# A weight conversion's closing integer addition on VectorE instead of GpSimd, in a fused attention and two-MLP kernel

## Chip, cores and metric

One core of a Trainium2 chip. The metric is the device time of one execution in microseconds: 691.84 us in the median of three runs before the change (691.09 to 692.73). Engines are named as in the profile: PE is TensorE, DVE is VectorE, ACT is ScalarE, POOL is GpSimd, SP is the engine that issues the DMAs.

## What is computed

Sliding-window attention with four sink columns, 2 batches x 8 heads x 768 positions x 64, then two MLPs over the 1536 tokens (512 -> 2048 -> 512 each) with two different activations. The MLP weights arrive as 64-bit floats.

```python
scores = scale * np.matmul(q, k.transpose(0, 1, 3, 2))
keep = is_sink | in_window                      # 4 sinks, window 128
a = softmax(np.where(keep, scores, -1e9))       # + 1e-9 in the denominator
x = np.matmul(a, v)                             # -> (1536, 512)
h = x @ w1_in                                   # first MLP
g = np.where(h >= 1, h, np.where(h <= -1, 0.0, (h + 1) ** 2 / 4.0))
x = g @ w1_out
h = x @ w2_in                                   # second MLP
g = h * np.clip(h + 3.0, 0.0, 6.0) / 6.0
out = g @ w2_out
```

## The kernel before

All data is kept transposed: features lie on the 128 partitions, tokens along the free dimension. Each matrix product of the MLPs is made of three passes on TensorE, because each operand is held as a high and a low part: high x high, high x low, low x high. The two parts are made by `high` (a copy that rounds to the matmul type, L139 to L145) and `low` (a DVE subtraction, L147 to L150).

The tokens are worked off in chunks (`CHUNKS`, L25): 512, 256, 256 and 512 tokens for the first MLP, three of 512 for the second. A chunk takes 16 steps, one per 128 of the 2048 hidden features (`FC`). In step s, `h_group(s)` (L537) makes 12 matmuls into one PSUM bank, then ACT and DVE apply the activation and split the result into gh and gl; two steps later `y_group` (L573) makes 12 matmuls of gh, gl and the output weights into four banks that accumulate over the 16 steps.

A weight tile is 128 x 512; there are 64: 16 for the way in and 16 for the way out of each MLP (raw0i, raw0o, raw1i, raw1o by the profile's names; 0 is the first MLP). A tile comes as 128 x 512 x 2 int32, the lower and upper words of the 64-bit floats. `narrow` (L179) makes an fp32 tile of it by integer work: L187 (ACT) or L185 (DVE) drops the sign of the upper word, L190 (DVE) clamps the value's range, L191 (DVE) takes the sign out of the upper word, L192 (DVE) shifts by 3 and puts the sign back, L195 (ACT) turns the lower word into a small number, and L196, the line that is changed, adds the two as integers. Two slots after `narrow`, `split` (L209) makes the high part (L143, ACT, or L145, DVE) and, a slot later, the low part (L150).

The order is set in three ways. PE and SP run in the order in which the program is written (`manual_schedule`, L630). For ACT, DVE and POOL, a planner orders the instructions. The program itself defers work: `defer(fn, slots)` keeps a function for so many slots, and `tick` (L126), which runs at each attention step and at each quarter of a step, calls those that are due; so the addition is written one slot after the rest of `narrow`. Where an operation can be made by ACT or DVE, `Balance` (L44) picks the engine whose account is less full; `bal.add` puts a known cost on an engine's account.

Attention is written as a list of small functions (`steps`), and `attend` calls them between the matmul groups: for chunk 0 before any MLP step, for the chunks 1 to 3 during the chunk before. The conversions of the first MLP's weights begin during the attention of chunk 0 (the way in runs eight steps ahead, `AHEAD`) and go on during chunk 0, one tile for the way in and one for the way out per step; the second MLP's are spread over chunk 3 of the first MLP and chunk 0 of the second (the queue of L608 to L615), as far as four raw buffers (`RAW`) and the weight tiles of the first MLP come free. After its conversion, an output-weight tile is written to DRAM (L213) and is read back by the later chunks (L227). The raw tile's last reader is L196, so SP's next load into that buffer (L173) waits for it.

Of the kernel before, what the change touches and what calls it, by code (L numbers as in the profile page):

```python
# [13 lines left out]
ALU = mybir.AluOpType  # L14
# [56 lines left out]
def f32(ap):  # L71
    return ap.bitcast(F32)
# [3 lines left out]
def sink_attention_moe_moe_kernel(  # L76
# [14 lines left out]
    nc = tc.nc  # L91
# [31 lines left out]
    def defer(fn, slots=1):  # L123
        waiting.append((clock[0] + slots, fn))
# [12 lines left out]
    bal = Balance()  # L137
# [41 lines left out]
    def narrow(t, dst):  # L179

        lo, hi = t[:, :, 0], t[:, :, 1]
        c = dst.bitcast(I32)
        n = c.shape[1]
        if bal.pick(dve=150 + n / 1.92, act=150 + n / 1.2) == "dve":
            nc.vector.tensor_scalar(out=c, in0=hi, scalar1=0x7FFFFFFF, scalar2=None, op0=ALU.bitwise_and)  # L185
        else:
            nc.scalar.activation(out=f32(c), in_=f32(hi), func=AF.Abs)  # L187
        bal.add("dve", 3 * 150 + 2 * n / 1.92 + n / 0.96)
        bal.add("act", 150 + n / 1.2)
        nc.vector.tensor_scalar(out=f32(c), in0=f32(c), scalar1=F64_LOW, scalar2=F64_HIGH, op0=ALU.max, op1=ALU.min)  # L190
        nc.vector.tensor_scalar(out=hi, in0=hi, scalar1=-(1 << 31), scalar2=None, op0=ALU.bitwise_and)  # L191
        nc.vector.scalar_tensor_tensor(  # L192
            out=c, in0=c, scalar=3, in1=hi, op0=ALU.logical_shift_left, op1=ALU.bitwise_xor
        )
        nc.scalar.activation(out=f32(lo), in_=lo.bitcast(U32), func=AF.Copy, scale=2.0 ** -51, bias=2.0)  # L195
        defer(lambda: nc.gpsimd.tensor_tensor(out=c, in0=c, in1=lo, op=ALU.add))  # L196

    def take(m, which, fc):

        t = raw.pop((m, which, fc))  # L200
        if which == "i":
            hi = wpool.tile([P, DM], F32R, tag=f"wih{fc}", name=f"wih{m}_{fc}")
            lo = wpool.tile([P, DM], F32R, tag=f"wil{fc}", name=f"wil{m}_{fc}")
            wi[m, fc] = (hi.rearrange("p (k f) -> p k f", f=P), lo.rearrange("p (k f) -> p k f", f=P))
        else:
            w = wo_tile(m, fc)
            hi, lo = w[:, 0, :], w[:, 1, :]

        def split(src):  # L209
            high(hi, src, DM)  # L210
            defer(lambda: low(lo, src, hi, DM))
            if which == "o":
                defer(lambda: nc.sync.dma_start(out=f32(wo_d[m][fc]), in_=f32(w.rearrange("p a f -> p (a f)"))), 4)  # L213

        if wide:
            t32 = raw_p.tile([P, DM], F32, tag="w32", name="w32", bufs=3)
            narrow(t, t32)
            defer(lambda: split(t32), 2)
        else:
            split(t)  # L220
# [409 lines left out]
    with tc.manual_schedule(engines={mybir.EngineType.PE, mybir.EngineType.SP}):  # L630
        nc.vector.memset(half, 0.5)
        make_identity(nc, ident)
        with ExitStack() as att:
# [17 lines left out]
            for s in range(len(seq) + LAG):  # L651
                lo = hi = fc = 0
                if s < len(seq):
                    ci, fc = seq[s]
                    m = chunks[ci][0]
                    if fast and ci + 1 < NCH:
                        lo, hi = ready[ci], ready[ci + 1]
# [65 lines left out]
```

## Time and profile before

| what | value |
|---|---|
| device time, median of 3 | 691.84 us (691.09 to 692.73) |
| the profiled execution's own time | 690.73 us |
| its span, from first to last instruction | 688.6 us |
| PE busy | 656.1 us, 95% |
| DVE busy | 429.2 us, 62% |
| ACT busy | 337.0 us, 49% |
| POOL busy | 97.7 us, 14% |
| mean granted clock of PE | 0.982 |
| chain that ended last | PE 78%, DVE 12%, DMA 6%, ACT 2% |

Busy time is the time in which an engine executes instructions. The chain is followed back from the last instruction: at each step to what released it, or to the instruction ahead of it on its engine. The profile's page has also the span in 40 slices with the busy share of each in tenths; DVE's line reads 5979998997765556553679999579322222222222, and POOL's 2311432332100000000113333133000000000000: there are two stretches in which both work.

### The profile page before, as it was taken

Reading aid. Unit: us, or ns where it says so; the run is one execution under the profiler, and the core shown is the slowest. Engines: PE = TensorE matmul, PEld = TensorE weight load, DVE = VectorE, ACT = ScalarE, POOL = GpSimd, SP = SyncE. Lnnn points to the kernel's source line nnn. Section 1 sums busy time; section 2 is a strip of 40 time slices with the busy share of each in tenths; the row PEclk is TensorE's granted clock in tenths of the full one; section 3 lists DMA queues with packets and bytes.
Section 4 is the critical chain, followed back from the end, with each engine's and each line's share of the span. In section 5 each row is a group of like instructions: output and inputs, shape, how many; then the busy total and the mean of one; then the engine's idle time right before and its main releaser. Section 6 shows DMA issues by size and latency. Waiting matters only on the chain.

```text
span 688.6 us, 9625 instructions
## 1 busy us (share of the span) xinstructions
PE 656.1 (95%) x3392; PEld 522.8 (76%) x3392; DVE 429.2 (62%) x968; ACT 337.0 (49%) x710; POOL 97.7 (14%) x83
## 2 busy tenths in 40 slices
PE   6889689989999999999999999999999999999997
PEld 3455457657788998888888887888888888888886
DVE  5979998997765556553679999579322222222222
ACT  6669756664454446554356566466232222222222
POOL 2311432332100000000113333133000000000000
PEclk9989889999999999999999999999999999999999
DMA  8135547834577465443199551994318332062321
GB/s 272 66 105 167 196 149 239 274 110 141 160 288 255 150 235 192 142 151 114 48 360 356 184 204 49 376 393 171 122 47 323 106 107 91 31 214 94 104 78 62
DMA packets 47024, 119.21 MB, mean 173 GB/s; under 512 B 4432, under 2 KB 15744, under 8 KB 46976
## 3 DMA queue, kind: packets, MB, share of 16 engines
q1 hardware_dynamic: 46976, 118.60, 49.5%
q8 instruction: 27, 0.44, 0.3%
q14 instruction: 21, 0.17, 0.1%
HBM read 92.36 MB, written 26.21 MB: 172 GB/s over the span
## 4 chain that ended last, share of the span: by engine, by line
PE 78%; DVE 12%; DMA 6%; ACT 2%; SPq 1%; issue 1%; POOL 0%; ACTq 0%; DVEq 0%; POOLq 0%
PE ps_y L589 34%; PE ps_h L545 34%; PE ps_v L421 5%; PE ps_s L321 3%; DVE w L192 2%; DMA raw0i<-moe_w_in_dram 2%; DVE w L190 2%; DMA raw0o<-moe_w_out_dram 1%; DVE p L328 1%; DVE wo L150 1%; PE ps_t L385 1%; PE ps_t L384 1%; DMA wo<-wo_d 1%; DVE wil L150 1%; DVE raw0i L191 1%; DVE p L342 1%
## 5 line engine op out<-in xcount | busy, mean ns | idle before, releaser
L589 PE MATMUL ps_y<-gh,wo 128*128 128x512 f32 (+1 forms) x896 | 268.8, 364 | 0.9 <-ACT pt L366 0.6
L589 PEld LDWEIGHTS ps_y<-gh,wo 128*128 128x128 f32 x896 | 163.5, 189 | 31.3 <-issue 4.6
L545 PE MATMUL ps_h<-xh,wih 128*128 128x512 f32 (+1 forms) x448 | 166.6, 372 | 11.0 <-DVE gl L150 11.0
L545 PE MATMUL ps_h<-xl,wih 128*128 128x512 f32 (+1 forms) x448 | 162.1, 362 | 0.4 <-DVE xl L150 0.4
L545 PE MATMUL ps_h<-xh,wil 128*128 128x512 f32 (+1 forms) x448 | 161.9, 361 | 0.0
L589 PE MATMUL ps_y<-gl,wo 128*128 128x512 f32 (+1 forms) x448 | 161.2, 360 | 0.0
L150 DVE TENSOR_TENSOR gl<-ps_h,gh 128x512 fp32r<-128x512 f32 (+1 forms) x112 | 68.6, 613 | 91.4 <-ACT gh L143 90.9
L143 ACT ACTIVATE gh<-ps_h 128x512 fp32r<-128x512 f32 (+1 forms) x112 | 60.0, 536 | 130.3 <-PE ps_y L589 91.8
L545 PEld LDWEIGHTS ps_h<-xh,wih 128*128 128x128 f32 x448 | 85.2, 190 | 31.6 <-DVE gl L150 13.0
L545 PEld LDWEIGHTS ps_h<-xl,wih 128*128 128x128 f32 x448 | 85.2, 190 | 12.8 <-DVE xl L150 0.9
L545 PEld LDWEIGHTS ps_h<-xh,wil 128*128 128x128 f32 x448 | 85.1, 190 | 12.9
L589 PEld LDWEIGHTS ps_y<-gl,wo 128*128 128x128 f32 x448 | 84.8, 189 | 12.0
L559 DVE SCALAR_TENSOR_TENSOR ps_h<-r,ps_h 128x512 f32<-128x512 f32 x48 | 33.4, 695 | 83.0 <-ACT r L558 82.9
L558 ACT ACTIVATE r<-ps_h,half 128x512 f32<-128x512 f32 x48 | 33.0, 688 | 87.5 <-PE ps_h L545 87.5
L347 ACT ACTIVATE p<-p,nm 128x260 f32<-128x260 f32 (+2 forms) x96 | 46.5, 485 | 30.1 <-DVE nm L328 29.5
L321 PE MATMUL ps_s<-kraw,qraw 64*128 64x260 f32 (+2 forms) x192 | 48.3, 475 | 13.2 <-DVE nm L328 7.3
L555 DVE SCALAR_TENSOR_TENSOR r<-r 128x512 f32<-128x512 f32 (+1 forms) x64 | 47.7, 745 | 14.9 <-ACT r L554 14.7
L196 POOL TENSOR_TENSOR w<-w,raw1i 128x512 int32<-128x512 int32 x16 | 24.8, 1547 | 209.6 <-ACT wih L143 145.6
L190 DVE TENSOR_SCALAR w<-w 128x512 f32<-128x512 f32 x64 | 40.1, 626 | 13.4 <-ACT w L187 13.3
L328 DVE CUSTOM_DVE_ANT_0 p<-ps_s,mask 128x260 f32<-128x260 f32 (+2 forms) x96 | 36.7, 398 | 17.0 <-PE ps_s L321 16.8
L321 PEld LDWEIGHTS ps_s<-kraw,qraw 64*128 64x128 f32 x192 | 23.4, 217 | 29.9 <-DVE nm L328 15.2
L554 ACT ACTIVATE r<-ps_h,half 128x512 f32<-128x512 f32 (+1 forms) x64 | 36.6, 571 | 15.9 <-PE ps_h L545 15.5
(60 smaller groups left out, 666.6 us busy)
## 6 DMA issues: line engine op xcount, KB each, us to landing
wo<-wo_d SPq DMA_DIRECT2D x80, 512.0 KB, 4.2
wo_d<-wo SPq DMA_DIRECT2D x32, 512.0 KB, 6.0
raw0i<-moe_w_in_dram SPq DMA_DIRECT2D x16, 512.0 KB, 5.5
raw0o<-moe_w_out_dram SPq DMA_DIRECT2D x16, 512.0 KB, 5.0
raw1i<-moe_w_in_dram SPq DMA_DIRECT2D x16, 512.0 KB, 5.9
raw1o<-moe_w_out_dram SPq DMA_DIRECT2D x16, 512.0 KB, 3.3
xh<-x2h_d SPq DMA_DIRECT2D x3, 1024.0 KB
xl<-x2l_d SPq DMA_DIRECT2D x3, 1024.0 KB, 9.3
```

What stands on the lines that cost most here:

```text
L143: nc.scalar.activation(out=dst, in_=src, func=AF.Copy)
L150: nc.vector.tensor_tensor(out=dst, in0=src, in1=f32(hi), op=ALU.subtract)
L190: nc.vector.tensor_scalar(out=f32(c), in0=f32(c), scalar1=F64_LOW, scalar2=F64_HIGH, op0=ALU.max, op1=ALU.min)
L321: nc.tensor.matmul(banks[e], tq[rows, u * P:(u + 1) * P], tk[rows, c0:c0 + w], start=True, stop=True)
L328: nc.vector.tensor_tensor_reduce(out=p[:, e, :], in0=banks[e], in1=masks[min(i, 2)], scale=-SCALE, scalar=BIG, op0=ALU.add, op1=ALU.min, a ...
L347: nc.scalar.activation(out=p[:, e, :], in_=p[:, e, :], func=AF.Exp, scale=-1.0, bias=nm[:, e:e + 1], accum_out=sm[:, e:e + 1],)
L421: nc.tensor.matmul(ps[e * D:(e + 1) * D, u0 * P:u1 * P], l, r, start=n == 0, stop=n == len(ops[0]) - 1)
L545: nc.tensor.matmul(ps, w[:, kc, :], x[:, kc, :], start=i == 0, stop=i == len(ops) - 1)
L554: nc.scalar.activation(out=r, in_=ps, func=AF.Relu, scale=0.5, bias=half)
L555: nc.vector.scalar_tensor_tensor(out=r, in0=r, scalar=1.0, in1=r, op0=ALU.min, op1=ALU.mult)
L559: nc.vector.scalar_tensor_tensor(out=ps, in0=r, scalar=1.0, in1=ps, op0=ALU.min, op1=ALU.mult)
L589: nc.tensor.matmul(ys[dm], a[:, cs], b, start=fc == 0 and i == 0, stop=fc == FC - 1 and i == 2)
```

## The change

The addition of L196 is issued to VectorE, and the planner's account of VectorE is charged for it. Nothing else is changed; the operands, the slot and all other lines are the same.

```diff
         nc.scalar.activation(out=f32(lo), in_=lo.bitcast(U32), func=AF.Copy, scale=2.0 ** -51, bias=2.0)
-        defer(lambda: nc.gpsimd.tensor_tensor(out=c, in0=c, in1=lo, op=ALU.add))
+        bal.add("dve", 160 + 1.3 * n)
+        defer(lambda: nc.vector.tensor_tensor(out=c, in0=c, in1=lo, op=ALU.add))
```

## Rows read from the trace of the kernel before

**Rows 1.** Table of two stretches: busy us (count) of PE, PEld, DVE, ACT, POOL

```profile
205.00:688.60 483.60, 478.80 (x2572) 400.85 (x2570) 254.78 (x523) 203.33 (x403) 43.33 (x29) 1.00 0.48 171
0.00:205.00 205.00, 177.34 (x823) 121.91 (x824) 174.39 (x446) 133.70 (x307) 54.37 (x54) 0.94 0.54 179
```

**Rows 2.** The same table, five stretches within the first 205 us

```profile
10.00:27.00 17.00, 14.19 (x40) 7.23 (x38) 16.19 (x50) 14.12 (x37) 4.43 (x4) 1.00 0.36 131
53.00:64.00 11.00, 9.90 (x54) 5.58 (x52) 10.65 (x38) 10.11 (x27) 2.67 (x2) 0.84 0.43 140
74.00:99.50 25.50, 16.54 (x65) 11.18 (x64) 25.14 (x47) 17.50 (x33) 10.58 (x8) 0.87 0.56 177
107.00:123.70 16.70, 16.48 (x78) 12.36 (x76) 15.86 (x30) 11.87 (x23) 5.91 (x4) 1.00 0.79 272
129.50:142.00 12.50, 8.40 (x40) 6.31 (x38) 12.50 (x25) 8.87 (x17) 5.40 (x4) 0.98 0.64 193
```

**Rows 3.** DVE instructions by line: count, duration ns minimum/median/maximum, start, forms

```profile
L190 DVE TENSOR_SCALAR w<-w x64: 400/421/1533, 10.9 to 477.8; 128x512 f32<-128x512 f32 x64
...
L192 DVE SCALAR_TENSOR_TENSOR w<-w,raw0i x16: 676/682/1774, 12.5 to 128.9; 128x512 int32<-128x512 int32 x16
...
L150 DVE TENSOR_TENSOR wil<-w,wih x32: 671/684/1806, 19.6 to 417.8; 128x512 fp32r<-128x512 f32 x32
...
L339 DVE TENSOR_SCALAR sm<-sm x48: 140/169/1274, 6.6 to 312.6; 128x2 f32<-128x2 f32 x48
...
L559 DVE SCALAR_TENSOR_TENSOR ps_h<-r,ps_h x48: 680/696/697, 424.4 to 677.5; 128x512 f32<-128x512 f32 x48
```

**Rows 4.** Timeline of POOL and DVE: start us, us, engine, line, instruction

```profile
17.38 1.29 POOL L196 TENSOR_TENSOR w<-w,raw0i 128x512 int32<-128x512 int32 x1 [2.77 <-ACT wih L143]
...
17.45 1.77 DVE L192 SCALAR_TENSOR_TENSOR w<-w,raw0i 128x512 int32<-128x512 int32 x1
...
79.60 0.68 DVE L192 SCALAR_TENSOR_TENSOR w<-w,raw0o 128x512 int32<-128x512 int32 x1
...
80.20 0.68 DVE L555 SCALAR_TENSOR_TENSOR r<-r 128x512 f32<-128x512 f32 x1
```

**Rows 5.** Table of stretches for line L196 alone: POOL busy us and (count)

```profile
0.00:205.00 205.00, 50.99 (x35) 0.94 0.54 179
...
330.00:500.00 170.00, 43.33 (x29) 1.00 0.62 229
```

**Rows 6.** DVE by line and form, 0 to 205 us, last row 205 to 330 us

```profile
L190 DVE TENSOR_SCALAR w<-w 128x512 f32<-128x512 f32 x35 | 22.4, 639 | 10.6 <-ACT w L187 10.6
...
L150 DVE TENSOR_TENSOR wo<-w,wo 128x512 fp32r<-128x512 f32 x16 | 14.3, 893 | 0.0
...
L192 DVE SCALAR_TENSOR_TENSOR w<-w,raw0i 128x512 int32<-128x512 int32 x16 | 13.5, 846 | 0.0
...
L150 DVE TENSOR_TENSOR wil<-w,wih 128x512 fp32r<-128x512 f32 x16 | 12.6, 788 | 0.0
...
L342 DVE TENSOR_SCALAR p<-p,sm 128x260 f32<-128x260 f32 x32 | 11.9, 413 | 0.1
...
L339 DVE TENSOR_SCALAR sm<-sm 128x2 f32<-128x2 f32 x30 | 9.1, 305 | 2.1 <-ACT p L347 2.0
...
L342 DVE TENSOR_SCALAR p<-p,sm 128x260 f32<-128x260 f32 x32 | 10.3, 352 | 0.5
```

**Rows 7.** Chain of waits within the first 205 us: start us, us, engine, tile, line

```profile
13.60 1.29 DVE w L190
...
138.39 0.85 DVE w L190
```

**Rows 8.** Waits in the first 205 us: who waited for whom, us, times, longest

```profile
ACT wo L143 <- POOL w L196: 9.9, 9, 3.0
...
PE ps_h L545 <- DVE gl L150: 10.3, 4, 5.9
...
SPq L173 <- POOL w L196: 20.0, 9, 4.8
```

## The prediction

> **What bounds the kernel now.** I read the page first, then a table of stretches, the chain of waits, and last the DVE instructions by kind. In the table of two stretches the reader sees where PE's idle time is: from 205 us on PE is busy for 478.80 of 483.60 us, before that for only 177.34 of 205.00 [rows 1]. So 27.7 us of idle time lie in the first 205 us, in which the first layer's weights are converted beside attention, and 4.8 us in all the rest. In the rest the chain is matmuls behind matmuls, 2.72 us per dozen once attention is over. Nothing that DVE saves there can show, as long as it keeps up.
>
> In the first 205 us DVE is busy for 174.39 us [rows 1], and the chain runs along DVE in long pieces. Five stretches of this kind, from 10, 53, 74, 107 and 129.5 us on, are 82.7 us in sum, and DVE is busy in 80.34 of them [rows 2]. Here VectorE's own work decides, and here 64 more instructions for VectorE look like a bad idea.
>
> What speaks for the change is how long DVE's instructions are. L190, the clamp, takes 421 ns in the median and up to 1533; L192 682 and up to 1774; the low half of a weight (L150, wil) 684 and up to 1806; even L339, on two columns, 169 and up to 1274 [rows 3]. The long ones lie beside a GpSimd addition: the one that starts at 17.38 runs 1.29 us, to 18.67, and L192, which starts at 17.45, takes 1.77 us instead of 0.68 and ends at 19.22, about its own usual time after the addition [rows 4]. It did not run slower, it stood still. L559, which reads one of its operands from PSUM, takes 680 to 697 ns in all 48 cases [rows 3], six of them beside an addition.
>
> The Trainium skill states this as a rule ("SBUF — State Buffer", Who interferes with whom): VectorE and GpSimd share a pair of ports, and the second to start waits for the whole of the first's instruction, where VectorE's is in a two-port mode or has two inputs in SBUF and GpSimd's reads SBUF. By that rule each stall goes with its addition, and the stall in the trace agrees.
>
> **What the change removes.** It removes 64 GpSimd additions, 35 of them before 205 us, of 50.99 / 35 = 1.46 us in the mean [rows 5], and the stalls that they cause. I size these by kind for the first 205 us: count times (mean there less undisturbed length) [rows 3, 6]. L190: 35 x (639 - 421) = 7.6 us. L339: 30 x (305 - 169) = 4.1. L150 wo: 16 x (893 - 684) = 3.3. L192 of raw0i: 16 x (846 - 682) = 2.6. L342 of 260 columns: 32 x (413 - 352, its mean from 205 to 330 us, where GpSimd is idle) = 2.0. L150 wil: 16 x (788 - 684) = 1.7. That is 21.3 us; L555, L191 and the narrower L342 bring it to about 27, worked out in the same way: 0.77 us per addition.
>
> **What it adds.** One VectorE instruction per weight tile, with two int32 tiles of 128x512 in SBUF as inputs. The trace has no such DVE addition. The nearest rows are L192 (int32, two SBUF inputs, 682 ns) and L150 (fp32, two SBUF inputs, 684) [rows 3], and I take 0.68 us. From below it is bounded by L190's 0.42 us with one input [rows 3], from above by the 1.46 us of the same addition on GpSimd. An instruction occupies the engine for less than its length, as the next starts before it ends: the 0.68-us ones at 79.60 and 80.20 are 0.60 apart [rows 4]. So 35 x 0.60 = 21 us come and 27 go, and DVE gets 6 us freer before 205 us. At the bounds (0.34 or 1.38 us occupied) it would be 15 us freer or 21 us fuller.
>
> **What of it is on the path.** In the five stretches led by DVE, 22 additions start (4 + 2 + 8 + 4 + 4) [rows 2]: 22 x 0.60 = 13.2 us are added to the chain. The chain now holds 18 stretched DVE pieces there; the first and the last are L190 at 13.60 with 1.29 us and at 138.39 with 0.85 us, against 0.34 undisturbed [rows 7]. Their excess is 16.5 us, 0.92 each. So these stretches shrink by 16.5 - 13.2 = 3.3 us. Outside of them two stretched L190 and one addition on GpSimd leave the chain and some three of DVE's join it, which I set at 0.5 us. The sum is 3.8 us.
>
> From 330 to 500 us the other 29 additions go the same way [rows 5]. A step of the first layer needs of DVE, undisturbed, L190 0.42 + L191 0.42 + L192 0.68 + the addition 0.68 + the low half 0.68 + three instructions of 0.69 for g (L555, L556, L150) = 4.95 us, and PE needs 2 x 2.72 = 5.44 us for that step. The cover is thin, 0.49 us, but the stalls that fill it now leave. I cost this part at nothing; without the cover 29 x 0.60 = 17 us are at stake.
>
> **The planner's account.** `bal.add` charges VectorE 826 ns per tile, which pushes choices to ScalarE. They are there already: all copies of L143 run on ACT, and of the 64 first steps of a conversion 63 are ACT's (L187) and one is DVE's (L185). At most that one moves, 0.4 us.
>
> **The hand-over.** Today GpSimd starts 0.13 to 0.23 us after L192's end and takes 1.46 us, so the sum is there some 1.7 us after L192. ScalarE waits for it, 9.9 us in 9 places for wo before 205 us [rows 8]. On VectorE it is there 0.7 us after L192 if it follows at once. L195 doesn't hold it up: it ended before L192 in all 64 cases. DVE's queue may: it is worked off in order, and the addition is written one step later than L192, so that L328, L342, gl or a second tile's L190 to L192 may stand between, and these stand behind it in turn; PE and ACT wait for them. SP's loads of raw tiles wait 20.0 us for the addition, which reads a raw tile last [rows 8]; that wait turns into one for VectorE, and SP's order stays.
>
> The sum is made against the profiled execution: 690.73 - 3.8 = 686.9 us. The median of the runs shown, 691.84, lies 1.1 us higher, so I name 688.0 us.
>
> **Rivals.** (a) Transfers and PE's own order hide it. Between the stretches the chain passes through loads of raw tiles that SP issues only once PE has freed an attention buffer; if those are fixed in time, DVE is only earlier at a wait. For it: four of the stretches border on such a load. Against it: what SP waits for there is PE, and PE was held up by DVE before. Time: within 1.4 us of 691.8. Chance 0.18.
>
> (b) Slower: the addition sits late in DVE's order. ACT works in order too, so a copy that waits for the sum blocks gh and the exponentials behind it. It decides from the point where over 1.0 us (1.7 less 0.7) of other DVE work stands between L192 and the addition: two instructions of 0.60, or L190, L191 and L192 of a second tile (0.34 + 0.34 + 0.60 = 1.28). If each of the 22 tiles then costs 0.4 us more, that is 8.8 us, less the 3.8 gained: 697. If DVE's stalls had another cause than GpSimd, only the 13.2 us would remain: 705. For it: DVE has work in its queue nearly always in these stretches. Against it: GpSimd has nothing left that DVE could stand still for. Chance 0.22.
>
> The Trainium skill has a rule on the side of (b) ("Perfetto Trace Analysis", Optimizing Scalar/DVE Operations): where VectorE is saturated, moving work to ScalarE or even GpSimd may make sense; this change does the reverse. The same paragraph warns that it might not help between VectorE and GpSimd, for their shared port, and the stall shown above is a case of that warning.
>
> (c) More than forecast: all 27 us of stalls count, a part of the additions falls into DVE's idle time (30.6 us before 205), and PE's wait for gl, 10.3 us in 4 places [rows 8], shrinks with them: 8 to 10 us, so 682 to 684. Chance 0.10.
>
> **How the numbers follow.** The forecast has 0.50 (684.5 to 690.4), (a) 0.18, (b) 0.22, (c) 0.10. About 0.2%, 1.4 us, is what a measurement of this kernel can tell from no change. Faster by more: 0.50 + 0.10 = 0.60; within it: 0.18; slower: 0.22. The range goes from 681.5, just past (c), to 696, up to the milder half of (b).
>
> **What would show it.** Right: L190, L192, L150 with w and L339 all within 0.1 us of their medians; 64 DVE additions of 0.66 to 0.70 us; DVE's busy time, 429 us, down by 48 (27 before 205 us and some 21 after 330, sized alike) and up by 64 x 0.60 = 38, to about 420; PE's idle time in the first 205 us down by 3 to 5 us; PE without gaps after 330 us. Wrong: longer additions; ACT's wait for the sum above 15 us; a new PE wait for gl in 330 to 500 us. The prediction falls if DVE gets freer and the first 205 us do not get shorter.

## Result: 1.5% faster, two to three times what was forecast

The changed kernel takes 680.30 us in the median of four runs (678.59 to 683.12), beside 692.09 for the kernel before. The ratio on record is 0.9854, with a 95% interval of 0.9819 to 0.9889. It isn't the quotient of these two medians (0.983); it is that to some 690.4 us, where the kernel before lay in two later series (690.24 and 690.42). A comparison on another occasion, six runs of it, gave 682.51 beside 689.38 us, ratio 0.9882 (0.9845 to 0.9918). So the change takes 7 to 12 us off; 3.8 were forecast. The median of 680.3 lies 1.2 us below the range; the ratio, applied to the 691.84 us on which the forecast stands, gives 681.7, at its lower edge.

The profiled execution took 683.12 us (span 681.3), the longest of the four. The page's busy times, to be read beside those of the table before:

```profile
PE 657.6 (97%) x3392; PEld 523.7 (77%) x3392; DVE 415.9 (61%) x1031; ACT 336.4 (49%) x711; POOL 3.4 (0%) x19
```

DVE's busy time fell from 429.2 to 415.9 us although it has 64 instructions more (1031 against 968; the one at L185 has gone to ACT). POOL is left with 3.4 us. The instructions of [rows 3], in the same columns, and the addition, which now stands on L197 and is issued as a custom instruction on 16-bit halves:

```profile
L190 DVE TENSOR_SCALAR w<-w x64: 406/422/430, 11.3 to 470.1; 128x512 f32<-128x512 f32 x64
...
L192 DVE SCALAR_TENSOR_TENSOR w<-w,raw0i x16: 673/686/692, 12.9 to 129.5; 128x512 int32<-128x512 int32 x16
...
L150 DVE TENSOR_TENSOR wil<-w,wih x32: 668/686/694, 18.4 to 409.4; 128x512 fp32r<-128x512 f32 x32
...
L197 DVE CUSTOM_DVE_ANT_0 w<-raw0i,w x16: 679/686/690, 14.6 to 132.7; 128x1024 uint16<-128x1024 uint16 x16
```

The stalls are gone to the last one: L190's longest is 430 ns where it was 1533. The addition takes 0.69 us, as its nearest rows had it (0.68). By kind, for the first 205 us (columns as in [rows 6]; L339 is now L340):

```profile
L190 DVE TENSOR_SCALAR w<-w 128x512 f32<-128x512 f32 x35 | 14.8, 422 | 11.9 <-ACT w L187 11.8
...
L150 DVE TENSOR_TENSOR wo<-w,wo 128x512 fp32r<-128x512 f32 x16 | 11.0, 687 | 0.6 <-ACT wo L143 0.6
...
L340 DVE TENSOR_SCALAR sm<-sm 128x2 f32<-128x2 f32 x31 | 5.0, 163 | 2.0 <-ACT p L348 1.9
```

The clamp fell from 639 to 422 ns in the mean, the low half of wo from 893 to 687, L339 from 305 to 163. PE idles 19.0 of the first 205 us instead of 27.7 [rows 1]:

```profile
0.00:205.00 205.00, 185.98 (x879) 128.79 (x880) 169.64 (x496) 136.14 (x318) 3.38 (x19) 0.93 0.58 192
```

The waits that answer to [rows 8]:

```profile
PE ps_h L546 <- DVE gl L150: 5.0, 3, 3.7
...
ACT wo L143 <- DVE w L197: 2.9, 2, 2.0
...
SPq L173 <- DVE w L197: 29.8, 9, 6.8
```

ACT's wait for the sum of a wo tile went from 9.9 to 2.9 us and PE's for gl from 10.3 to 5.0. SP's wait for the raw tile's last reader grew from 20.0 to 29.8 us. SP comes to that point earlier: over the 16 steps its waits for PE, at the attention loads that it issues in between (L290 and L302 before), fell from 75.4 to 49.6 us.

The place of the gain is best seen with the span cut at the first matmul of a step: the start (up to step 0), the 16 steps of chunk 0, the 32 of chunks 1 and 2, the next 24 (chunk 3 and half of the chunk after it), and the rest. Before (columns as in [rows 1]: stretch, length, then PE, PEld, DVE, ACT, POOL, clock, DMA):

```profile
0.00:68.30 68.30, 55.90 (x240) 30.75 (x240) 55.79 (x204) 49.08 (x136) 15.17 (x28) 0.93 0.46 153
68.30:192.50 124.20, 108.94 (x505) 80.18 (x504) 109.75 (x221) 77.24 (x155) 37.65 (x25) 0.95 0.58 187
192.50:332.50 140.00, 139.69 (x1091) 120.87 (x1090) 79.11 (x267) 71.28 (x188) 1.54 (x1) 1.00 0.53 183
332.50:461.60 129.10, 128.36 (x578) 106.38 (x577) 108.71 (x170) 74.95 (x129) 35.24 (x23) 1.00 0.67 251
461.60:688.60 227.00, 223.25 (x985) 184.57 (x984) 75.82 (x110) 64.48 (x103) 8.09 (x6) 1.00 0.35 122
```

After:

```profile
0.00:74.10 74.10, 62.29 (x241) 33.71 (x241) 56.44 (x222) 52.20 (x141) 3.38 (x19) 0.82 0.43 142
74.10:185.10 111.00, 104.05 (x505) 77.95 (x504) 98.62 (x235) 72.31 (x149) 0.00 (x0) 0.98 0.63 205
185.10:325.10 140.00, 139.74 (x1092) 120.89 (x1091) 80.61 (x270) 71.98 (x190) 0.00 (x0) 1.00 0.53 185
325.10:454.40 129.30, 128.41 (x579) 106.44 (x578) 105.53 (x192) 75.00 (x128) 0.00 (x0) 1.00 0.67 250
454.40:681.30 226.90, 223.16 (x985) 184.67 (x983) 74.75 (x117) 64.87 (x104) 0.00 (x0) 1.00 0.35 122
```

The last three stretches differ by 0.0, 0.2 and 0.1 us. The 16 steps fell from 124.2 to 111.0 us, and the start got longer, 68.3 to 74.1. PE's idle time in the 16 steps went from 15.3 to 7.0 us, and PE was then busy for 94% of them. The other 4.9 us of the 13.2 are PE's busy time, 108.94 to 104.05 us for the same number of matmuls, at a granted clock of 0.98 instead of 0.95.

### The profile page after: what moved, and what is told of

Read it like the earlier page. It is cut to its first block, busy times and chain, and to the rows that moved or that the text cites. A ratio compares the mean times of both kernels' runs of the same rounds, so it can differ in the third digit from the quotient of the medians.

```text
span 681.3 us, 9471 instructions
## 1 busy us (share of the span) xinstructions
PE 657.6 (97%) x3392; PEld 523.7 (77%) x3392; DVE 415.9 (61%) x1031; ACT 336.4 (49%) x711; POOL 3.4 (0%) x19
## 4 chain that ended last, share of the span: by engine, by line
PE 74%; DVE 11%; DMA 9%; ACT 3%; issue 1%; SPq 1%; ACTq 0%
PE ps_y L590 32%; PE ps_h L546 31%; DMA raw0i<-moe_w_in_dram 4%; PE ps_s L322 4%; PE ps_v L422 4%; DVE w L192 2%; DMA raw0o<-moe_w_out_dram 2%; DVE w L197 2%; DMA raw1o<-moe_w_out_dram 1%; PE ps_t L386 1%; DMA raw1i<-moe_w_in_dram 1%; PE ps_t L385 1%; ACT w L187 1%; PE ps_k L397 1%; DVE p L329 1%
## 5 line engine op out<-in xcount | busy, mean ns | idle before, releaser
L590 PEld LDWEIGHTS ps_y<-gh,wo 128*128 128x128 f32 x896 | 163.1, 189 | 31.5 <-issue 4.4
L590 PE MATMUL ps_y<-gl,wo 128*128 128x512 f32 (+1 forms) x448 | 160.9, 359 | 0.0
L150 DVE TENSOR_TENSOR gl<-ps_h,gh 128x512 fp32r<-128x512 f32 (+1 forms) x112 | 68.7, 613 | 87.4 <-ACT gh L143 87.3
L546 PEld LDWEIGHTS ps_h<-xl,wih 128*128 128x128 f32 x448 | 84.9, 190 | 11.8
L322 PE MATMUL ps_s<-kraw,qraw 64*128 64x260 f32 (+2 forms) x192 | 50.0, 495 | 11.4 <-DVE nm L329 6.9
L329 DVE CUSTOM_DVE_ANT_0 p<-ps_s,mask 128x260 f32<-128x260 f32 (+2 forms) x96 | 36.8, 401 | 20.0 <-PE ps_s L322 19.8
L555 ACT ACTIVATE r<-ps_h,half 128x512 f32<-128x512 f32 (+1 forms) x64 | 36.7, 573 | 17.6 <-PE ps_h L546 17.1
L556 DVE SCALAR_TENSOR_TENSOR r<-r 128x512 f32<-128x512 f32 (+1 forms) x64 | 35.4, 554 | 15.5 <-ACT r L555 15.4
L190 DVE TENSOR_SCALAR w<-w 128x512 f32<-128x512 f32 x64 | 27.0, 422 | 17.1 <-ACT w L187 16.9
L557 DVE TENSOR_TENSOR ps_h<-ps_h,r 128x512 f32<-128x512 f32 (+1 forms) x64 | 35.9, 562 | 0.8
```

The lines of the kernel that those rows point to most:

```text
L150: nc.vector.tensor_tensor(out=dst, in0=src, in1=f32(hi), op=ALU.subtract)
L322: nc.tensor.matmul(banks[e], tq[rows, u * P:(u + 1) * P], tk[rows, c0:c0 + w], start=True, stop=True)
L329: nc.vector.tensor_tensor_reduce(out=p[:, e, :], in0=banks[e], in1=masks[min(i, 2)], scale=-SCALE, scalar=BIG, op0=ALU.add, op1=ALU.min, a ...
L546: nc.tensor.matmul(ps, w[:, kc, :], x[:, kc, :], start=i == 0, stop=i == len(ops) - 1)
L555: nc.scalar.activation(out=r, in_=ps, func=AF.Relu, scale=0.5, bias=half)
L556: nc.vector.scalar_tensor_tensor(out=r, in0=r, scalar=1.0, in1=r, op0=ALU.min, op1=ALU.mult)
```

## Experiments

Three theories stood against each other. **A**: the gain is that VectorE no longer stands still beside GpSimd. **B**: it is the planner's new order of DVE and ACT, which differs from the old one almost from the start. **C**: it is the hand-over, the sum and the raw tile being there sooner.

**The stalls put back, everything else kept (e1, e9).** After the VectorE addition GpSimd adds the sum to itself into a tile that nobody reads. In the programs, DVE's and ACT's instructions stand in the changed kernel's order one by one.

```diff
+        def add():
+            nc.vector.tensor_tensor(out=c, in0=c, in1=lo, op=ALU.add)
+            nc.gpsimd.tensor_tensor(out=spill, in0=c, in1=c, op=ALU.add)
+
+        defer(add)
-        defer(lambda: nc.vector.tensor_tensor(out=c, in0=c, in1=lo, op=ALU.add))
```

> The changed kernel, with one GpSimd addition more per weight tile: when VectorE has made the sum, GpSimd adds the sum to itself into a tile that nobody reads (same shape and type as the addition of the kernel before). The order of VectorE's and ScalarE's instructions is the changed kernel's, instruction for instruction. Theory A (the gain is that VectorE no longer stands still): the stalls come back, some 0.77 us per addition, 27 us on DVE before 205 us, of which 16.5 us lay on the chain: 680 + 16.5 = 697 us, and at least 688. Theory B (the gain is the planner's new order of DVE and ACT): the order is unchanged, so 680 us within 2. Theory C (the gain is that the sum is there sooner and the raw tile is released sooner): both are kept, so 680 us within 2.

Measured: 703.59 us (700.37 to 706.76), ratio 1.0193 (1.0148 to 1.0237) to the kernel before; that is 6.6 us over the 697 expected. e9 is the same with `[:, 0:2]` on the three operands of GpSimd's addition.

> As e1_pool_beside, but GpSimd's extra addition reads and writes 2 of the 512 columns. Waits, semaphores and the order of DVE and ACT are those of e1_pool_beside; only the length of GpSimd's work differs. Theory A (what costs is DVE standing still for as long as GpSimd works): some 0.1 to 0.2 us per addition, so 680 to 685 us. Rival (what made e1_pool_beside slow, 703.6 us, is the further reader of the sum, that is, buffers released later, and semaphores): 698 us or more.

Measured: 680.11 us (678.94 to 682.25), ratio 0.9868 (0.9817 to 0.9920). At one and the same order, with the same waits, 64 GpSimd additions of 512 columns (1.17 us in the mean) cost 703.59 - 680.11 = 23.5 us more than 64 of 2 columns (0.35 us). That is theory A, and B and C are out as explanations of this cost. The later release of the sum's tile is no cause either: in e1 ACT waits for GpSimd's addition once, for 0.5 us, in the whole span. The 23.5 us are not DVE's lost time alone, as PE's clock falls with it (see the table below). One stall in e1, on the timeline (start, length; L193 is L192 of the kernel before):

```profile
87.33 1.04 POOL L200 TENSOR_TENSOR spill<-w 128x512 int32<-128x512 int32 x1 [4.04 <-DVE w L199]
...
87.10 0.68 DVE L150 TENSOR_TENSOR gl<-ps_h,gh 128x512 fp32r<-128x512 f32 x1
87.70 1.21 DVE L193 SCALAR_TENSOR_TENSOR w<-w,raw0o 128x512 int32<-128x512 int32 x1
```

GpSimd works from 87.33 to 88.37. L193, with two inputs in SBUF, starts at 87.70 and ends at 88.91, half a microsecond later than it would. The gl subtraction, which reads one input from PSUM, keeps its 0.68 us beside the same addition, but it had started first. The trace of the kernel before shows the case in which GpSimd starts first:

```profile
96.86 1.58 POOL L196 TENSOR_TENSOR w<-w,raw0o 128x512 int32<-128x512 int32 x1 [4.78 <-DVE w L192]
97.23 0.68 DVE L150 TENSOR_TENSOR gl<-ps_h,gh 128x512 fp32r<-128x512 f32 x1
...
372.99 1.54 POOL L196 TENSOR_TENSOR w<-w,raw1i 128x512 int32<-128x512 int32 x1 [3.42 <-DVE w L192]
373.27 1.81 DVE L555 SCALAR_TENSOR_TENSOR r<-r 128x512 f32<-128x512 f32 x1
```

Ten gl subtractions of 512 columns start there with over 1.1 us of a GpSimd addition still to come, and none takes more than 0.69 us; of twelve L555, as large but with both inputs in SBUF, eleven take 1.79 to 1.81 us, and the twelfth stands beside an addition that itself takes 2.15 us instead of some 1.3. In both traces, 91 of the 93 DVE instructions that start within an addition and are over 0.1 us longer than usual are so by what GpSimd had left at their start, less 0.12 to 0.14 us. Where the difference lies, in the profiled executions of e1 and then of e9, which are 27.7 us apart (start, 16 steps, 24 steps):

```profile
0.00:76.80 76.80, 60.34 (x241) 32.08 (x241) 60.97 (x212) 51.30 (x139) 14.55 (x29) 0.87 0.42 137
76.80:202.50 125.70, 110.66 (x505) 81.46 (x504) 115.68 (x246) 76.25 (x153) 29.80 (x25) 0.93 0.55 182
...
342.00:477.00 135.00, 130.82 (x578) 107.29 (x578) 116.51 (x192) 74.63 (x128) 25.27 (x23) 0.99 0.65 239
```

```profile
0.00:69.70 69.70, 55.98 (x240) 30.75 (x240) 54.45 (x216) 50.13 (x138) 6.18 (x29) 0.90 0.46 150
69.70:181.10 111.40, 104.73 (x504) 77.64 (x503) 100.79 (x242) 74.24 (x154) 8.83 (x24) 0.98 0.62 205
...
321.10:450.10 129.00, 128.35 (x578) 106.40 (x577) 105.37 (x192) 74.92 (x128) 7.24 (x22) 1.00 0.68 251
```

The start differs by 7.1 us, the 16 steps by 14.3, the 24 steps by 6.0. The last is the thin cover of the prediction: with additions and stalls on DVE at once, the steps beside PE's 5.44 us no longer fit, and PE waits 4.1 us there for gl. Without the stalls it holds to about 1 us (129.0 to 129.5 us with the change, 129.1 before, 128.1 in e2 with no addition).

**No addition at all (e2), and two (e3).** e2 leaves the lower words out.

```diff
-        nc.vector.tensor_scalar(out=hi, in0=hi, scalar1=-(1 << 31), scalar2=None, op0=ALU.bitwise_and)
+        nc.vector.tensor_scalar(
+            out=hi, in0=hi, scalar1=-(1 << 31), scalar2=-(1 << 30), op0=ALU.bitwise_and, op1=ALU.bitwise_xor
+        )
...
-        defer(lambda: nc.gpsimd.tensor_tensor(out=c, in0=c, in1=lo, op=ALU.add))
```

> The kernel before without the addition on any engine: the lower words are left out, and the exponent is put right in L191 by a second bitwise operation instead. Neither GpSimd's stalls nor VectorE's additions are there. Theory A: against the changed kernel DVE has 21 us less before 205 us, of which 13 lie on the path: 680 - 13 = 667 us, and in any case below 680. Theory B: an order of its own, anywhere between 680 and 695. Theory C: the sum is there at once, so faster than 680 too, but DVE's busy time tells nothing of it.

Measured: 671.20 us (668.10 to 673.76), ratio 0.9722 (0.9686 to 0.9758), 4 us over the 667 of theory A. So GpSimd's additions cost the kernel before 690.24 - 671.20 = 19.0 us, waits for the sum included, and VectorE's cost the changed kernel 680.30 - 671.20 = 9.1 us; by the two intervals each is good to some 3 us.

e3 adds `nc.vector.tensor_tensor(out=spill, in0=c, in1=c, op=ALU.add)` behind the changed kernel's addition.

> The changed kernel with a second VectorE addition per tile, the sum with itself into a tile that nobody reads. It prices an addition of 0.60 us on VectorE. By the prediction's sum (22 of 35 on the path) 13.2 us more than the changed kernel, 693 us; if all 35 before 205 us count, 21 more, 701; if VectorE isn't what decides in the first 205 us, 680 within 2. The planner orders DVE and ACT anew here, which may add or take some us.

Measured: 691.09 us (688.80 to 693.75, ten runs), ratio 1.0010 (0.9992 to 1.0028): the second addition costs 10.8 us. That is less than the 13.2 of the sum on which it was tested, though not by more than the noise. e2 (start, 16 steps), then e3 (start, 16 steps, 24 steps):

```profile
0.00:63.90 63.90, 54.53 (x241) 30.12 (x241) 47.71 (x204) 48.20 (x134) 3.38 (x19) 0.87 0.49 157
63.90:177.00 113.10, 106.34 (x505) 78.90 (x504) 89.61 (x221) 75.68 (x157) 0.00 (x0) 0.95 0.63 208
```

```profile
0.00:74.30 74.30, 57.78 (x240) 31.28 (x240) 59.70 (x224) 50.74 (x138) 3.38 (x19) 0.91 0.43 142
74.30:189.40 115.10, 103.45 (x505) 75.89 (x503) 112.83 (x264) 76.55 (x155) 0.00 (x0) 1.00 0.62 206
330.60:462.10 131.50, 128.80 (x578) 106.31 (x577) 115.52 (x211) 74.61 (x128) 0.00 (x0) 1.00 0.65 243
```

The 16 steps take 113.1 us with no addition (DVE busy for 89.61), 111.0 with one (98.62), 115.1 with two (112.83). PE's idle time in them, which leaves out how long its matmuls take, is 6.8, 7.0 and 11.7 us. Up to one, no cost of the additions shows here; with two, DVE is busy for 98% of the stretch. In the start PE idles 9.4 us without additions and 11.8 with ten of them on VectorE (13.7 in e9). Each program has an order of its own, so these readings are good to some 2 us.

How many additions stand on the path can be counted in the chain of waits itself. In the changed kernel's first 205 us it holds 13 of the 34 that VectorE makes in the start and the 16 steps, 7.8 us; four of them lie in the start. Three of its twelve rows:

```profile
14.70 0.60 DVE w L197
...
126.14 1.20 DVE w L197 x2
...
151.70 0.60 DVE w L197
```

In the profile of the changed kernel's second series (e12, below) it is 15 additions and 9.0 us, in e9's 13 and 7.7 us. In e3, where DVE makes two per tile, it is 50 and 30.4 us. That is 22.6 us more than in the changed kernel, while the time grew by 10.8: to stand on the chain bounds what an addition can cost and isn't yet its cost.

What the chain passes through in the 16 steps, after the change and then before, as the view cuts the row off:

```profile
by line: DMA raw0i<-moe_w_in_dram 16.6%; PE ps_h L546 12.8%; PE ps_y L590 12.7%; DMA raw0o<-moe_w_out_dram 9.8%; DVE w L197 4.9%; DVE w L192 4.3%; issue 3.8%; ACT w L187 3.8%; DVE gl L150 2.9%; DVE wo L150 2.9%; DVE r L556 2.2%; DVE w L190 
```

```profile
by line: PE ps_h L545 11.7%; PE ps_y L589 9.2%; DVE w L192 8.5%; DMA raw0o<-moe_w_out_dram 8.2%; DVE w L190 8.1%; PE ps_v L421 5.6%; DVE wo L150 5.1%; DMA raw1i<-moe_w_in_dram 4.5%; DMA raw0i<-moe_w_in_dram 3.6%; DMA wo_d<-wo 3.6%; DVE gl L
```

Loads of raw0i and raw0o went from 11.8 to 26.4% of it, and all of DVE's pieces together from 51.6 to 31.4 us (40.9 in e12).

**PE's idle time and its clock.** Over the start and the 16 steps together, in the profiled executions, and the same number of matmuls within two:

| kernel | PE idle, us | PE busy, us |
|---|---|---|
| before | 27.7 | 164.8 |
| changed kernel, and e12 | 18.8 and 19.8 | 166.3 and 162.7 |
| e9 (GpSimd beside, 2 columns) | 20.4 | 160.7 |
| e1 (GpSimd beside, 512 columns) | 31.5 | 171.0 |
| e2 (no addition) | 16.1 | 160.9 |
| e3 (two on VectorE) | 28.2 | 161.2 |
| e10 and e13 (below) | 20.8 and 19.7 | 159.5 and 157.9 |

PE's idle time falls by 8 to 9 us with the change, in both of its profiles. PE's busy time differs by up to 13 us, as its granted clock does (0.82 in the changed kernel's start, 0.97 in e13's). About half of what parts e1 from e9 here is of this second kind, and so are one to two thirds of what parts e2 from the changed kernel's two profiles. Whether the clock is lower because of the idle time ahead of it was not tested.

**The halves (e4, e5).** `narrow` gets m as an argument, and VectorE adds for one MLP's tiles only.

```diff
+        if m == 0:                                   # e5: m == 1
+            bal.add("dve", 160 + 1.3 * n)
+            defer(lambda: nc.vector.tensor_tensor(out=c, in0=c, in1=lo, op=ALU.add))
+        else:
+            defer(lambda: nc.gpsimd.tensor_tensor(out=c, in0=c, in1=lo, op=ALU.add))
```

> VectorE makes the addition for the first MLP's 32 tiles alone, GpSimd that for the second's 32. Theory of the prediction (only what happens before 205 us counts): as the changed kernel, 680 us within 2, though DVE still stands still some 20 us between 330 and 500. Rival (the later additions count too): half of the gain, 686 us or more.

Measured: 681.16 us (677.77 to 682.72), ratio 0.9862 (0.9827 to 0.9897).

> The counterpart of e4_first_only: VectorE makes the addition for the second MLP's 32 tiles alone, GpSimd that for the first's. If only what happens before 205 us counts, the kernel before's time, 690.4 us within 2. Rival (the stalls between 330 and 500 us cost time too): 686 or less.

Measured: 689.64 us (687.71 to 693.06, ten runs), ratio 1.0009 (0.9985 to 1.0033). The whole gain that these runs can tell is made in the first MLP's conversions. That DVE stands still for some 20 us between 330 and 500 us costs nothing that shows beside their noise of some 2 us.

**The account (e6, e7).** e6 is the kernel before with the `bal.add` line, e7 the changed kernel without it.

> The kernel before with the line that charges VectorE's account alone; the addition stays on GpSimd. The prediction holds that the account moves one instruction at most: 690.2 us within 2. Rival (the account, by what it does to ACT's and DVE's share and to the planner's order, is a part of the gain): 686 or less.

Measured: 688.30 us against 690.42 (ten runs), ratio 0.9981 (0.9951 to 1.0012).

> The changed kernel without the line that charges VectorE's account. If that line does nothing but move one instruction, the changed kernel's 680 us within 2; e6_account_only (688.3 against 690.4 us, interval of the ratio 0.9951 to 1.0012) leaves open that it is worth some 2 us, then 682 to 683.

Measured: 681.64 us (680.88 to 682.40), ratio 0.9884 (0.9852 to 0.9916). By either run the account is worth some 2 us, and neither tells that from nothing. The gain is in the addition's move.

**The longer start (e11).** The first eight tiles are those that the start converts.

```diff
+        if early:                                    # m == 0 and which == "i" and fc < AHEAD
+            defer(lambda: nc.gpsimd.tensor_tensor(out=c, in0=c, in1=lo, op=ALU.add))
+        else:
             bal.add("dve", 160 + 1.3 * n)
             defer(lambda: nc.vector.tensor_tensor(out=c, in0=c, in1=lo, op=ALU.add))
```

> The changed kernel, with the first eight tiles' addition (those converted during the attention that comes before the first MLP step) back on GpSimd. In the profiles the first MLP step starts at 68.3 us before and at 74.1 and 71.5 us with VectorE's additions, while the 16 steps after it last 124.2 us before and 111.0 with the change. If both parts stand for themselves, the first part is worth 3 to 6 us here: 674 to 677 us. Rival (the later start is the planner's new order and not the additions): 680 to 684.

Measured: 682.85 us (679.70 to 684.41), ratio 0.9899 (0.9845 to 0.9953). No gain: my expectation was wrong, and the start was read wrongly. That it is 5.8 us longer can't all be put down to the change. Four programs with one order of DVE and ACT up to there begin step 0 at 74.1 (the changed kernel), 71.5 (e4), 70.6 (e12) and 69.7 us (e9), and the clock granted to PE over their starts is 0.82, 0.86, 0.88 and 0.90 of full. Two of the slices, first of the changed kernel, then of e9:

```profile
34.00:51.00 17.00, 14.79 (x61) 8.14 (x59) 12.29 (x50) 9.81 (x29) 0.00 (x0) 0.60 0.29 84
51.00:68.00 17.00, 14.90 (x71) 8.29 (x72) 14.33 (x56) 14.55 (x41) 0.00 (x0) 0.77 0.42 141
```

```profile
34.00:51.00 17.00, 14.47 (x66) 7.96 (x65) 12.82 (x53) 10.73 (x31) 0.39 (x2) 0.70 0.37 111
51.00:68.00 17.00, 13.32 (x77) 7.30 (x75) 15.30 (x60) 14.61 (x42) 0.78 (x2) 0.90 0.41 124
```

The clock, a mean between its levels of 1.2 and 2.4 GHz, is lower in the profile of the changed kernel, though PE was busy for 15.77 of the 17 us before these in both. So one profile's start is uncertain by 4 us. What grew from the kernel before to the changed one is PE's busy time in the start, 55.90 to 62.29 us for one matmul more; its idle time did not (12.4 and 11.8 us). How much of the 5.8 us goes with the change stays open: 1.4 (69.7 against 68.3) is the least of the four. Why the clock falls more in one execution than in another was not settled.

**A version with neither addition (e10, e13).** ScalarE makes the lower word's number negative, so that its bits hold the sign and exponent correction as well; the lower word is scaled by 15/16, so that it fits into the three bits that the shift leaves free, and it holds for weights below 2. L191 takes the sign and joins the lower word in one instruction.

```diff
-        nc.vector.tensor_scalar(out=hi, in0=hi, scalar1=-(1 << 31), scalar2=None, op0=ALU.bitwise_and)
+        nc.scalar.activation(out=f32(lo), in_=lo.bitcast(U32), func=AF.Copy, scale=-0.9375 * 2.0 ** -51, bias=-2.0)
+        nc.vector.scalar_tensor_tensor(
+            out=hi, in0=hi, scalar=-(1 << 31), in1=lo, op0=ALU.bitwise_and, op1=ALU.bitwise_xor
+        )
         nc.vector.scalar_tensor_tensor(
             out=c, in0=c, scalar=3, in1=hi, op0=ALU.logical_shift_left, op1=ALU.bitwise_xor
         )
-        nc.scalar.activation(out=f32(lo), in_=lo.bitcast(U32), func=AF.Copy, scale=2.0 ** -51, bias=2.0)
-        defer(lambda: nc.gpsimd.tensor_tensor(out=c, in0=c, in1=lo, op=ALU.add))
```

> A version that needs neither addition. ScalarE makes the lower word's number negative (-2 and a little), so that its bits hold the correction of the exponent too; L191 becomes one VectorE instruction that takes the sign of the upper word and joins the lower word to it bitwise, and L192 joins both to the shifted value. Per tile DVE has L190 0.34 + 0.60 + 0.60 = 1.54 us occupied, against 0.34 + 0.34 + 0.60 + 0.60 = 1.88 with the change and 0.94 less 0.34 for nothing in the kernel without an addition, so 0.26 us more than that one. By theory A: 671.2 us plus 0 to 35 x 0.26 = 9.1, so 672 to 679, faster than both. By a rival in which the time saved comes from the order alone, anywhere between 671 and 690. It holds for weights below 2 in magnitude, as all are here.

(The 0.94 in this text is wrong: the kernel without an addition, e2, occupies DVE for 0.34 + 0.34 + 0.60 = 1.28 us per tile.) Measured: 674.51 us (671.72 to 676.74), ratio 0.9782 (0.9727 to 0.9837). The new instruction and L192 (L195 here), in the first 205 us:

```profile
L192 DVE SCALAR_TENSOR_TENSOR raw0i<-raw0i 128x512 int32<-128x512 int32 x16 | 11.0, 686 | 0.1
...
L195 DVE SCALAR_TENSOR_TENSOR w<-w,raw0i 128x512 int32<-128x512 int32 x16 | 10.9, 684 | 0.0
```

It was then run beside the changed kernel.

> The changed kernel once more, for a comparison on one chip with the version without either addition: 680 us within 2. The start of the 16 steps, 74.1, 71.5 and 69.7 us in three programs with the same order of DVE and ACT up to there, should again follow the granted clock of the first 85 us.

> The version e10_fold once more, beside the changed kernel: 674.5 us within 2, that is, 5 to 6 us below the changed kernel. The rival (the two differ by no more than their scatter) would have them within 2 us.

Measured: 682.51 us (676.16 to 684.47, six runs; 0.5 outside what was expected) for the changed kernel and 676.20 us (672.65 to 677.36, five runs) for this version, ratios 0.9882 (0.9845 to 0.9918) and 0.9791 (0.9761 to 0.9821) to the same 17 runs of the kernel before. The version beats both, the changed kernel by 6.3 us. That this comes from DVE's shorter work, as theory A had it, is not shown: PE's idle time over the start and the 16 steps is no smaller than in the changed kernel (see the table). What is smaller is PE's busy time over the whole span, 650.4 and 648.8 us against 657.6 and 654.1, at a mean granted clock of 0.990 and 0.992 against 0.977 and 0.985; the 24 steps are 1.0 to 1.6 us shorter.

## Why the prediction was right in direction and short in size

- **What bounds.** Right: the gain lies before 205 us, and the last three stretches are unchanged (e4, e5).
- **Stalls removed.** Right in kind and size. All long instructions are gone, and DVE's busy time came to 415.9 us where some 420 was named. On the path 16.5 us and a little outside were counted; e2 measures 19.0 with the waits for the sum, and e1 against e9, less the 6.0 us of the 24 steps, 17.5. That these lie so near 16.5 is in part luck: both hold a change of PE's clock, which the sum didn't have, and e1's additions are other ones (1.17 us in the mean instead of 1.46).
- **Price of one addition.** Right: 0.68 us was taken, 0.69 measured, though in another form of instruction than was thought.
- **Additions on the path.** This is the step that failed: "22 x 0.60 = 13.2 us are added to the chain", and three more outside. The chain of the changed kernel holds 13 of them, 7.8 us (13 to 15 and up to 9.0 us in the other profiles), not 25 and 15 us, and the measured cost of all additions is 9.1 us. The stretches in which DVE led were read from a chain that the stalls had made. With the stalls gone, DVE leads in less of the 16 steps: its pieces on the chain there went from 51.6 to 31.4 us (40.9 in e12), and the chain passes instead through loads of raw tiles (raw0i and raw0o, 26.4% of the stretch, 11.8% before). An addition beside such a load is not on the path. A net of 17 - 13 was a small difference of two large terms; with 19.0 - 9.1 it is 9.9. The sum had no term for PE's clock either; PE's busy time differs by up to 13 us between these profiles.
- **The cover after 330 us.** Right, and as thin as said: it holds with the addition, and breaks in e1 by 6.0 us and in e3, with two additions, by 2.2.
- **The account.** Right within what can be told: one instruction moved.
- **The hand-over.** The feared delay did not come: ACT's wait for the sum fell. How much of e2's 19.0 us is this wait and how much the stalls was not separated.
- **Rivals.** (b), the slower one, fails on the changed kernel itself: VectorE's queue is as feared, and ACT's wait for the sum fell. (a) is wrong as an outcome, but its limit, loads that SP issues late, is what appears behind DVE now. (c), "a part of the additions falls into DVE's idle time", had the mechanism of the part that failed and nearly the size (682 to 684), at a chance of 0.10. Its other half, that all 27 us of stalls count, isn't shown: 17 to 19 are measured.

Open: whether more raw buffers would shorten the 16 steps, and how much of the gain is PE's clock. Neither was tried.

## What to carry to other kernels

An instruction moved onto a full engine can make that engine emptier, if the place it came from blocked it: compare the maximum with the median of each kind of instruction on the full engine before counting its load. When such stalls go, the chain that they made goes too, so what is added can't be priced on the chain in the profile of before: price it once as if all of it counted and once as if only a part did, and let the range hold both. And where the forecast is a small difference of two large terms, its range should take in what comes if either is off by a third.

## Not expected of the hardware

- A VectorE instruction on two columns (L339, 169 ns in the median) stood still for as long as one on 512: up to 1274 ns before, never after. The reciprocal behind it (L340), on the same two columns, never did: 168 ns at the most, in five cases within an addition.
- The 32-bit integer addition on VectorE appears as one instruction on 128x1024 16-bit elements and takes 0.69 us, as long as an fp32 subtraction of two tiles of that size (L150).
- The same work of DVE and ACT in the same order takes 69.7 to 74.1 us up to step 0, with PE's granted clock over that stretch between 0.90 and 0.82.
